# Experts of a fused attention and mixture kernel: side work, first weight fetches and last sums re-spaced

## The chip, the cores and the metric

The kernel runs on one core of one Trainium2 chip. The metric is device time in microseconds; the median of three runs of the kernel before is 872.75 us (871.38 to 873.23). Engines: PE (TensorE matmul), PEld (its weight loads), DVE (Vector), ACT (Scalar), POOL (GpSimd), SP (Sync, here the queue that issues DMAs).

## The reference

Three layers follow one another: gated linear attention over 4 x 8 heads of 768 steps, a mixture of 8 experts with equal capacity (3072 tokens, 384 each), and a dense layer with a cosine gate.

```python
def _moe_ref(x, w_gate, w1, w2):
    logits = x @ w_gate
    order = np.argsort(-logits.flatten())        # best (token, expert) pairs first
    # a pair is taken if the token is free and the expert has fewer than N // E tokens
    ...
    for e in range(E):
        mask = assigned == e
        h = np.maximum(x[mask] @ w1[e], 0.0)     # 384 -> 1024
        out[mask] = h @ w2[e]                    # 1024 -> 384

def _moe2_ref(x, w_in, w_out):
    h = x @ w_in                                 # 384 -> 2048
    g = h * np.cos(h)
    return (g @ w_out).astype(np.float32)        # 2048 -> 384
```

`w_in` and `w_out` are scaled with a numpy float64 and so reach the kernel as 64-bit floats; the kernel takes them as pairs of 32-bit words and makes float32 of them with integer operations.

## The kernel before

The kernel has three stages: attention (up to about 168 us in the profile), the search for the first full expert (up to about 180 us), and `experts`, which this change is about. The order in which experts fill up is found on the way: a search finds the next expert to be full and its threshold, and the tokens of that expert are then fixed. The kernel works through the experts in that order, 384 tokens at a time, and does the routing of the next expert beside the matmuls of the current one.

**Precision.** Every float32 product is three matmuls (`mm3`, lines 741 to 743, and lines 811 to 813): operands are split into a rounded high part (made on ACT, `..h`) and the rest (made on DVE or POOL, `..l`). A piece of work on PE in this text is nine matmuls of 128x384.

**One expert.** `prefetch` gathers the tokens with three indirect DMAs on POOL (line 706, one per 128 tokens), and fetches the first three of eight raw weight blocks on SP (line 716, three buffers). `convert` makes a block's high part on ACT (`wh`, line 723) and low part on POOL (`wl`, line 724; the first three of the first expert on DVE), and then fetches the block three further on. `xpose` transposes the tokens on PE (line 753). `up(f)` is the first product for block f of 1024/128 = 8 with its relu (`hh` on ACT, `hl` on DVE), `down(f)` the second, into `accB`. `up2(f)` is the third product for one of 16 blocks of 2048 with the cosine (ACT, DVE, ACT, DVE), then `gh` on ACT and `gl` on POOL (lines 800, 801), and `down2(f)` the last product into `accD`, which runs three blocks behind `up2`. The last `down2` of an expert copies `accD` out and scatters the rows with an indirect DMA on POOL (line 820).

**Side work.** The generator `beside` of expert n yields the routing of expert n + 1, its `prefetch` and its first five conversions, step by step. `tick` is called 42 times in an expert, after each piece of matmuls or so, and takes the next step on two calls of three. A search has six refinement steps k. In each, DVE compares all best logits with a list of thresholds (`C`, line 549, in two halves), PE counts (`cn`, line 545), DVE decides whether the capacity is reached (`less`, `sat`), PE adds up (`num`, line 572), and DVE makes the next thresholds (`thr`, lines 589 and 597). `C` and its count are one step of the generator, the decision and the new thresholds the next. Experts 0 to 5 have a search beside them (for experts 1 to 6); expert 6 has only the routing of the last expert, and expert 7 nothing. Behind the search come the ranks (`rk`, line 632), four comparisons `L` (line 661), their product `xi` (line 658) and the indices `idx` (line 675).

**Late weights.** Ten of the 16 blocks of `w_out` are converted during attention; the last six (`LATE`) beside the first expert by `convert_late`. Each has four steps: an absolute value on ACT (line 137), two operations on DVE (lines 139, 140), two more on DVE (142, 143), and the high part on ACT with the low part on POOL (146, 147). `next(late, None)` takes one step.

**What sets the order.** Program order is a priority. When the program is built, a planner simulates the engines with its own costs and gives every engine a fixed list: of the instructions that it takes to be ready, the earliest in program order. `in_order` pins an engine's list to program order: POOL and DVE in the lead-in of `experts`, ACT in the main loop. On the chip each engine works through its list and waits where an input is not there. The lead-in (from line 830) routes expert 0, calls `prefetch`, converts five blocks, keeps PE running with matmuls that nobody reads (`busy`, 22 in a row and two after each third of the transposes) and transposes.

Of the kernel before, what the change touches and what calls it, by code (L numbers as in the profile page):

```python
# [525 lines left out]
def search(nc, K, rp, ps, Z, n, em, found):  # L526
    V, PE = nc.vector, nc.tensor
    mx, oh = Z["mx"], Z["oh"]
    steps = FIRST if n == 0 else LATER
    thr, tau, old = K["t0"].bitcast(F32)[:, ::2 ** (steps[0] - 25)], None, None  # L530
    for k, st in enumerate(steps):
        T = 2 ** ((32 if k == 0 else steps[k - 1]) - st)
        g = P // T if n > 0 else 1
        if st:
            nx = steps[k + 1]
            wd = 2 ** (st - nx)
        if k == 0 and n == 0:
            cn = Z["cn"]
        else:
            C = rp.tile([P, NU, T], BF16, name="C", tag="C")  # L540
            cn = ps.tile([g * T, g * E], F32, name="cn", tag="rt")

            def count(a, z):
                for c in range(a, z, g):
                    PE.matmul(cn, C[:, c:c + g].rearrange("p c t -> p (c t)"), oh[:, c:c + g].rearrange("p c e -> p (c e)"), start=(c == 0), stop=(c == NU - g))  # L545

            cuts = (0, 15, NU) if n == 0 else tuple(range(0, NU + 1, HALF))
            for a, z in zip(cuts, cuts[1:]):
                V.tensor_tensor(C[:, a:z], mx[:, a:z, None].to_broadcast([P, z - a, T]), thr[:, None, :].to_broadcast([P, z - a, T]), op=ALU.is_ge)  # L549
                if n == 0:  # L550
                    count(a, z)
            if n > 0:
                count(0, NU)
            if st and k:
                base = rp.tile([P, wd], I32, name="base", tag="base")
                V.scalar_tensor_tensor(base, K["io"][:, :wd], nx, tau.to_broadcast([P, wd]), op0=ALU.logical_shift_left, op1=ALU.bitwise_xor)
            yield
        sat = rp.tile([T, E], BF16, name="sat", tag="sat")
        if g == 1:
            V.tensor_scalar(sat, cn, CAP - 0.5, None, op0=ALU.is_ge)  # L560
        else:
            less = None
            for j in range(1, g):
                part = cn[j * T:(j + 1) * T, j * E:(j + 1) * E]
                more, less = less, rp.tile([T, E], F32, name="less", tag="less", bufs=2)
                if j == 1:
                    V.tensor_scalar(less, part, -1.0, None, op0=ALU.mult)
                else:
                    V.scalar_tensor_tensor(less, part, -1.0, more, op0=ALU.mult, op1=ALU.add)
            V.scalar_tensor_tensor(sat, cn[:T, :E], 0.5 - CAP, less, op0=ALU.add, op1=ALU.is_ge)  # L570
        num = ps.tile([P, E], F32, name="num", tag="rt")
        PE.matmul(num, K["onesb" if st == 0 else "ones0"][:T], sat, start=True, stop=True)
        ix = rp.tile([P, 1], I32, name="ix", tag="ix")
        if st == 0:
            top = rp.tile([P, 1], F32, name="top", tag="top")
            V.tensor_reduce(top, num, axis=AX, op=ALU.max)
            sel = rp.tile([P, E], F32, name="sel", tag="sel")
            V.scalar_tensor_tensor(sel, num, top, K["eb"], op0=ALU.is_equal, op1=ALU.mult)
            V.tensor_reduce(em, sel, axis=AX, op=ALU.max)
            V.tensor_scalar(ix, top, -1.0, None, op0=ALU.add)  # L580
            V.tensor_tensor(found, ix, tau, op=ALU.bitwise_xor)
            yield
            break
        with nc.allow_low_precision(reason="small whole numbers"):
            V.tensor_reduce(ix, num, axis=AX, op=ALU.max)
        old, tau = tau, rp.tile([P, 1], I32, name="tau", tag="tau", bufs=2)
        if k:
            thr = rp.tile([P, wd], I32, name="thr", tag="thr", bufs=2)
            V.scalar_tensor_tensor(thr, ix.to_broadcast([P, wd]), st, base, op0=ALU.logical_shift_left, op1=ALU.bitwise_xor)
            V.scalar_tensor_tensor(tau, ix, st, old, op0=ALU.logical_shift_left, op1=ALU.bitwise_xor)  # L590
        else:
            t2 = rp.tile([P, 1], I32, name="t2", tag="t2i")
            V.tensor_scalar(tau, ix, st, -2**31, op0=ALU.logical_shift_left, op1=ALU.bitwise_xor)
            V.tensor_scalar(t2, tau, 31, 0x7FFFFFFF, op0=ALU.arith_shift_right, op1=ALU.bitwise_and)
            V.tensor_tensor(tau, tau, t2, op=ALU.bitwise_xor)
            thr = rp.tile([P, wd], I32, name="thr", tag="thr", bufs=2)
            V.scalar_tensor_tensor(thr, K["io"][:, :wd], nx, tau.to_broadcast([P, wd]), op0=ALU.logical_shift_left, op1=ALU.bitwise_xor)  # L597
        thr = thr.bitcast(F32)
        yield
    if n == 0:  # L600
        V.tensor_copy(Z["ems"], em)
    else:
        V.tensor_tensor(Z["ems"], Z["ems"], em, op=ALU.add)
# [84 lines left out]
def experts(tc, nc, ctx, K, R, Z, xs, wcat, wout, out):  # L688
# [13 lines left out]
    def prefetch(r):  # L702
        r["xg"] = []
        for j in range(3):
            t = mp.tile([P, HD], F32, name="xg", tag="xg", bufs=3)
            GP.indirect_dma_start(out=t, out_offset=None, in_=xs, in_offset=bass.IndirectOffsetOnAxis(ap=r["idx"][:, j:j + 1], axis=0))
            r["xg"].append(t)
        r["e"] = nc.sync.value_load(r["es"][0:1, 0:1], min_val=0, max_val=E - 1)
        r["raw"], r["w"] = {}, {}
        for f in range(3):  # L710
            fetch(r, f)

    def fetch(r, f):
        if f < NA:
            r["raw"][f] = mp.tile([P, 2 * HD], F32, name="raw", tag="raw", bufs=3)
            nc.sync.dma_start(r["raw"][f], wcat[bass.ds(r["e"], 1), :, f].rearrange("a p c -> p (a c)"))

    def convert(r, f, eng=None):
        if f < NA:
# [110 lines left out]
    late = convert_late(nc, mp, R, wout)  # L830
    next(late)
    cur = fresh()
    second = fresh()
    steps = route(nc, K, rp, rtp, Z, 1, second)
    with in_order(tc, nc, (mybir.EngineType.Pool, mybir.EngineType.DVE)):
        for _ in route(nc, K, rp, rtp, Z, 0, cur):
            pass
        prefetch(cur)
        for f in range(5):
            convert(cur, f, V if f < 3 else None)  # L840
        next(steps)
        cur["busy"] = mmp.tile([P, 512], F32, name="busy", tag="mm")
        busy(cur, 22)
        xpose(cur, 2)
        mark = {i.name for i in nc.cur_bb.bb.instructions}
    up(cur, 0)
    up(cur, 1)
    with in_order(tc, nc, (mybir.EngineType.Activation,)):
        for n in range(E):
# [3 lines left out]
            def beside():  # L853
                if nxt is not None:
                    if n == 0:
                        next(steps)
                        hold(tc, nc, mybir.EngineType.DVE, mark)
                        yield
                    yield from steps if n == 0 else route(nc, K, rp, rtp, Z, n + 1, nxt)
                    prefetch(nxt)  # L860
                    yield
                    for f in range(5):
                        convert(nxt, f)
                        yield
            side = beside()
            count = [0]

            def tick():
                count[0] += 1
                if count[0] % 3:  # L870
                    next(side, None)
            for f in range(2, NA):
                up(r, f)
                tick()
                down(r, f - 2)
                convert(r, f + 3)
                tick()
            for d in range(3):
                down(r, NA - 2, (d,))
# [6 lines left out]
            for f in range(LEAD, LAG):  # L886
                up2(r, f)
                next(late, None)
                tick()
                next(late, None)  # L890
            down2(r, (0,))
            tick()
            for f in range(LAG, NF):
                up2(r, f)
                next(late, None)
                tick()
                down2(r, (f - LAG + 1,))
                next(late, None)
                tick()
            for f in range(NF + 1 - LAG, NF - 2):  # L900
                down2(r, (f,))
                tick()
            for _ in side:
                pass
            if nxt is not None:
                xpose(nxt)
                down2(r, (NF - 2,))
                up(nxt, 0)
                up(nxt, 1)
                down2(r, (NF - 1,))  # L910
            else:
                down2(r, (NF - 2, NF - 1))
            cur = nxt


# [93 lines left out]
```

## Time and profile before

| | |
|---|---|
| median of 3 runs | 872.75 us |
| profiled execution | 871.95 us |
| its span | 870.2 us |
| PE busy | 810.0 us (93%) |
| DVE busy | 529.8 us (61%) |
| ACT busy | 423.8 us (49%) |
| POOL busy | 378.8 us (44%) |
| raw fetch, median from issue to landing | 3.4 us (64 of 384 KB) |

Busy time is the time in which the engine has an instruction running; matmuls overlap, so a busy PE is not yet PE at its peak. The granted clock of PE is full (2.4 GHz) or half of that (1.2 GHz); the views give it as a share. The times in the views count from the start of the span. In a row of a windows view the busy times stand in the order PE, PEld, DVE, ACT, POOL, each with its number of instructions.

### The profile page before, as it was taken

What the parts mean: (1) busy time and instruction counts of PE and PEld (TensorE: products, weight loads), DVE (VectorE), ACT (ScalarE), POOL (GpSimd) and SP (SyncE); (2) the same over time, 40 slices, a digit from 0 to 9 for tenths busy, and PEclk for the clock granted to TensorE, in tenths of its full rate; (3) what the DMA queues carried; (4) which work ended last, traced back from release to release, by engine and by line L of the source; (5) the groups of instructions that cost most, each with busy time, mean ns of one, the idle gap of its engine ahead of it and who ended that gap; (6) DMA issues with size and microseconds to landing.
All of it is one profiled execution on the core that took longest, in us unless ns stands there. A gap on an engine that the chain in (4) does not pass through costs nothing.

```text
span 870.2 us, 15619 instructions
## 1 busy us (share of the span) xinstructions
PE 810.0 (93%) x5886; PEld 760.0 (87%) x5886; DVE 529.8 (61%) x1365; ACT 423.8 (49%) x814; POOL 378.8 (44%) x329
## 2 busy tenths in 40 slices
PE   6989999648998899999999999999999999999996
PEld 4878889527988889999998999899989999999996
DVE  5888888565697368546844683567357645432332
ACT  4777776113355425632563356245624553753552
POOL 5545555013146513751384138314732563734233
PEclk9999999859999999999999999999999999999999
DMA  9988884142032201220131014002300133300000
GB/s 243 262 229 222 232 223 120 40 126 86 1 109 82 83 1 55 72 75 2 55 101 46 1 55 119 28 1 73 101 28 27 60 113 85 92 1 28 1 2 28
DMA packets 27348, 71.91 MB, mean 83 GB/s; under 512 B 4608, under 2 KB 7936, under 8 KB 27264
## 3 DMA queue, kind: packets, MB, share of 16 engines
q1 hardware_dynamic: 24192, 61.38, 24.7%
q0 software_dynamic: 3072, 9.44, 3.4%
q8 instruction: 49, 0.80, 0.4%
q14 instruction: 35, 0.29, 0.1%
HBM read 61.37 MB, written 9.44 MB: 81 GB/s over the span
## 4 chain that ended last, share of the span: by engine, by line
PE 47%; DVE 2%; ACT 1%; issue 0%; POOL 0%; POOLq 0%; ACTq 0%
PE accD L812 5%; PE accD L811 5%; PE accD L813 5%; PE pC L742 5%; PE pC L741 5%; PE pC L743 5%; PE accB L741 2%; PE pA L741 2%; PE accB L742 2%; PE accB L743 2%; PE pA L743 2%; PE pA L742 2%; DVE C L549 1%; DVE thr L597 1%; PE xtp L753 1%; PE cn L545 1%
## 5 line engine op out<-in xcount | busy, mean ns | idle before, releaser
L801 POOL TENSOR_TENSOR gl<-ki,gh 128x384 fp32r<-128x384 f32 x128 | 132.1, 1036 | 249.8 <-ACT gh L800 228.1
L813 PE MATMUL accD<-woh,gl 128*128 128x384 f32 x384 | 131.1, 341 | 5.6 <-POOL gl L801 5.6
L724 POOL TENSOR_TENSOR wl<-raw,wh 128x768 fp32r<-128x768 f32 x61 | 112.7, 1853 | 51.4 <-ACT wh L723 43.5
L811 PE MATMUL accD<-woh,gh 128*128 128x384 f32 x384 | 131.7, 343 | 0.5 <-ACT gh L800 0.5
L812 PE MATMUL accD<-wol,gh 128*128 128x384 f32 x384 | 130.9, 341 | 0.0
L743 PE MATMUL pC<-yTh,wil 128*128 128x384 f32 x384 | 130.3, 339 | 0.0
L741 PE MATMUL pC<-yTh,wih 128*128 128x384 f32 x384 | 130.0, 341 | 0.0
L742 PE MATMUL pC<-yTl,wih 128*128 128x384 f32 x384 | 129.9, 338 | 0.0
L787 DVE SCALAR_TENSOR_TENSOR ki<-pC,ki 128x384 f32<-128x384 f32 x128 | 71.0, 555 | 85.2 <-ACT ki L785 85.0
L785 ACT ACTIVATE ki<-pC,quarter 128x384 int32<-128x384 f32 x128 | 73.7, 576 | 92.2 <-PE pC L743 90.9
L792 DVE TENSOR_TENSOR ki<-pC,ki 128x384 f32<-128x384 f32 x128 | 71.0, 555 | 53.8 <-ACT ki L790 50.3
L790 ACT ACTIVATE ki<-ki,halfpi 128x384 f32<-128x384 f32 x128 | 79.0, 617 | 43.9 <-DVE ki L787 43.6
L732 ACT ACTIVATE hh<-pA 128x384 fp32r<-128x384 f32 x64 | 31.5, 492 | 114.9 <-PE pA L743 114.9
L723 ACT CAST wh<-raw 128x768 fp32r<-128x768 f32 x64 | 52.3, 828 | 61.6 <-PE accB L742 32.2
L813 PEld LDWEIGHTS accD<-woh,gl 128*128 128x128 f32 x384 | 72.7, 189 | 7.3 <-POOL gl L801 7.2
L733 DVE SCALAR_TENSOR_TENSOR hl<-pA,hh 128x384 fp32r<-128x384 f32 x64 | 35.5, 555 | 63.1 <-ACT hh L732 62.9
L811 PEld LDWEIGHTS accD<-woh,gh 128*128 128x128 f32 x384 | 72.8, 189 | 0.9 <-ACT gh L800 0.8
L742 PEld LDWEIGHTS pC<-yTl,wih 128*128 128x128 f32 x384 | 72.5, 189 | 0.6 <-DVE yTl L736 0.5
L800 ACT CAST gh<-ki 128x384 fp32r<-128x384 f32 x128 | 64.8, 506 | 16.8 <-DVE ki L792 16.6
L812 PEld LDWEIGHTS accD<-wol,gh 128*128 128x128 f32 x384 | 72.6, 189 | 0.0
L741 PEld LDWEIGHTS pC<-yTh,wih 128*128 128x128 f32 x384 | 72.5, 189 | 0.1
L743 PEld LDWEIGHTS pC<-yTh,wil 128*128 128x128 f32 x384 | 72.5, 189 | 0.0
(187 smaller groups left out, 1688.8 us busy)
## 6 DMA issues: line engine op xcount, KB each, us to landing
raw<-in_wcat_dram SPq DMA_DIRECT2D x64, 384.0 KB, 3.4
ring<-in_qk_dram SPq DMA_DIRECT2D x48, 192.0 KB, 5.0
vf<-in_qkvf_dram SPq DMA_DIRECT2D x23, 384.0 KB, 4.9
wr<-in_win_dram SPq DMA_DIRECT2D x12, 512.0 KB, 5.4
xs<-xx SPq DMA_DIRECT2D x24, 192.0 KB, 2.7
wr<-in_wout_dram SPq DMA_DIRECT2D x10, 384.0 KB, 4.8
lr<-in_wout_dram SPq DMA_DIRECT2D x6, 384.0 KB, 3.3
vf<-in_qkvf_dram SPq DMA_DIRECT2D x2, 192.0 KB, 3.2
```

The costliest lines, as they stand in the source:

```text
L724: (eng or GP).tensor_tensor(l, raw, h.bitcast(F32), op=ALU.subtract)
L741: PE.matmul(o, ah, bh, start=first, stop=False)
L742: PE.matmul(o, ah, bl, start=False, stop=False)
L743: PE.matmul(o, al, bh, start=False, stop=last)
L785: SC.activation(ki, p, AF.Identity, bias=quarter, scale=INV2PI)
L787: V.scalar_tensor_tensor(fr, p, INV2PI, ki, op0=ALU.mult, op1=ALU.subtract)
L790: SC.activation(fr, fr, AF.Sin, bias=halfpi, scale=TWO_PI)
L792: V.tensor_tensor(g, p, fr, op=ALU.mult)
L801: GP.tensor_tensor(gl, g, gh.bitcast(F32), op=ALU.subtract)
L811: PE.matmul(r["accD"][t], gh[:, s], R["oh"][:, f], start=(f == 0), stop=False)
L812: PE.matmul(r["accD"][t], gh[:, s], R["ol"][:, f], start=False, stop=False)
L813: PE.matmul(r["accD"][t], gl[:, s], R["oh"][:, f], start=False, stop=(f == NF - 1))
```

## The change

- In `search`, a step with n > 0 yields once more, between `C` and its count.
- `tick` takes a side step on every call. A conversion in `beside` yields twice.
- In the first expert, fetches of raw blocks 3 and later (`fetch`, f >= 3) wait for the third gather. SP issues them.
- Two of the steps of `convert_late` now come with each block of the up and down loop, and one, not two, with each block of up2. The number of calls up to block 12 of up2 is 24 in both versions.
- 18 instead of 22 `busy` matmuls stand ahead of the transposes.
- In the last expert, `down2` of block 13 is no longer a call by itself: blocks 13, 14 and 15 are summed in one call, all three for the first 128 tokens, then for the second, then for the third.

```diff
@@ search
                 if n == 0:
                     count(a, z)
             if n > 0:
+                yield
                 count(0, NU)
             if st and k:
                 base = rp.tile([P, wd], I32, name="base", tag="base")
@@ prefetch, fetch
         for j in range(3):
             t = mp.tile([P, HD], F32, name="xg", tag="xg", bufs=3)
-            GP.indirect_dma_start(out=t, out_offset=None, in_=xs, ...)
+            got = GP.indirect_dma_start(out=t, out_offset=None, in_=xs, ...)
             r["xg"].append(t)
         r["e"] = nc.sync.value_load(r["es"][0:1, 0:1], min_val=0, max_val=E - 1)
         r["raw"], r["w"] = {}, {}
         for f in range(3):
             fetch(r, f)
+        if r.get("wait"):
+            r["wait"] = got.ins
 
     def fetch(r, f):
         if f < NA:
             r["raw"][f] = mp.tile([P, 2 * HD], F32, name="raw", tag="raw", bufs=3)
-            nc.sync.dma_start(r["raw"][f], wcat[...])
+            d = nc.sync.dma_start(r["raw"][f], wcat[...])
+            if f >= 3 and r.get("wait"):
+                info = mybir.DependencyInfo(mybir.DependencyClass.Sync, mybir.DependencyReason.DATA)
+                tc.add_manual_dep(d.ins, r["wait"].name, info, reason="gathers first")
@@ lead-in
     cur = fresh()
+    cur["wait"] = True
...
-        busy(cur, 22)
+        busy(cur, 18)
@@ main loop
                     for f in range(5):
                         convert(nxt, f)
                         yield
+                        yield
             side = beside()
-            count = [0]
 
             def tick():
-                count[0] += 1
-                if count[0] % 3:
-                    next(side, None)
+                next(side, None)
             for f in range(2, NA):
                 up(r, f)
+                next(late, None)
                 tick()
                 down(r, f - 2)
                 convert(r, f + 3)
+                next(late, None)
                 tick()
...
                 up2(r, f)
                 next(late, None)
                 tick()
-                next(late, None)
             down2(r, (0,))
             tick()
             for f in range(LAG, NF):
                 up2(r, f)
                 next(late, None)
                 tick()
                 down2(r, (f - LAG + 1,))
-                next(late, None)
                 tick()
-            for f in range(NF + 1 - LAG, NF - 2):
+            for f in range(NF + 1 - LAG, NF - 2 if nxt is not None else NF - 3):
                 down2(r, (f,))
                 tick()
...
             else:
-                down2(r, (NF - 2, NF - 1))
+                down2(r, (NF - 3, NF - 2, NF - 1))
```

## Rows read from the trace of the kernel before

**Rows 1.** Windows by expert (first, third): stretch, length, busy us (instructions), clock, DMA share, GB/s.
```profile
200.77:293.41 92.64, 84.67 (x501) 79.10 (x501) 67.20 (x167) 44.99 (x85) 41.12 (x34) 0.96 0.22 66
376.36:459.62 83.26, 81.53 (x510) 77.60 (x510) 50.34 (x141) 38.70 (x71) 36.73 (x30) 1.00 0.18 53
```

**Rows 2.** Windows: late stretch of the first and third expert, then the first's up stretch.
```profile
263.39:290.84 27.45, 21.64 (x101) 20.01 (x100) 17.76 (x24) 16.05 (x30) 20.88 (x17) 0.88 0.35 100
439.76:457.05 17.29, 17.29 (x100) 17.26 (x100) 6.14 (x11) 12.44 (x22) 16.50 (x14) 1.00 0.46 127
...
200.50:228.00 27.50, 26.50 (x174) 24.26 (x174) 17.99 (x51) 7.19 (x13) 6.41 (x4) 1.00 0.10 29
```

**Rows 3.** Waits of PE from 200 us on: us in total, times, longest.
```profile
PE cn L545 <- DVE C L549: 7.4, 7, 1.3
PE accD L813 <- POOL gl L801: 5.6, 4, 2.8
PE rk L632 <- DVE R L630: 0.6, 1, 0.6
```

**Rows 4.** Timeline, third expert: start, us, engine, line, operation, [idle before, releaser].
```profile
388.68 1.84 POOL L724 TENSOR_TENSOR wl<-raw,wh 128x768 fp32r<-128x768 f32 x1 [1.70 <-ACT wh L723]
...
388.83 1.77 DVE L597 SCALAR_TENSOR_TENSOR thr<-io,tau 128x64 int32<-128x64 int32 x1
...
389.64 0.33 PE L741 MATMUL accB<-hh,wh 128*128 128x384 f32 x1
...
390.63 1.83 DVE L549 TENSOR_TENSOR C<-mx,thr 128x768 bf16<-128x768 f32 x2
391.64 0.31 PE L545 MATMUL cn<-oh,C 128*128 128x16 bf16 x6 [1.32 <-DVE C L549]
...
393.20 0.35 PE L741 MATMUL pA<-xTh,wh 128*128 128x384 f32 x1
```

**Rows 5.** Timeline of PE, third expert, around two later counts.
```profile
397.21 0.34 PE L743 MATMUL pA<-xTh,wl 128*128 128x384 f32 x1
397.60 0.24 PE L545 MATMUL cn<-oh,C 128*128 128x32 bf16 x3
...
415.79 0.34 PE L813 MATMUL accD<-woh,gl 128*128 128x384 f32 x1
416.23 0.24 PE L545 MATMUL cn<-oh,C 128*128 128x32 bf16 x3
```

**Rows 6.** Line 597, the thresholds: count, ns min/median/max, first and last start, forms.
```profile
L597 DVE SCALAR_TENSOR_TENSOR thr<-io,tau x7: 193/1769/1775, 168.1 to 638.1; 128x64 int32<-128x64 int32 x6, 128x32 int32<-128x32 int32 x1
```

**Rows 7.** Tile `lv`, the late blocks' DVE steps: count, ns min/median/max.
```profile
L139 DVE TENSOR_SCALAR lv<-lv x6: 342/350/1090, 237.8 to 274.6; 128x384 f32<-128x384 f32 x6
L140 DVE TENSOR_SCALAR lv<-lv x6: 339/346/1867, 238.3 to 275.7; 128x384 int32<-128x384 int32 x6
L142 DVE SCALAR_TENSOR_TENSOR lv<-lr,lv x6: 543/932/1261, 239.1 to 277.6; 128x384 int32<-128x384 int32 x6
L143 DVE SCALAR_TENSOR_TENSOR lv<-lr,lv x6: 536/543/545, 240.1 to 279.3; 128x384 int32<-128x384 int32 x6
```

**Rows 8.** Timeline of the lead-in; a later gather; the window after that.
```profile
192.33 9.23 SPq L716 DMA_DIRECT2D raw<-in_wcat_dram  x5
...
194.30 1.08 POOL L706 DMA_INDIRECT xg<-xs,idx  x1 [0.30 <-issue]
...
199.65 0.55 PE L753 MATMUL xtp<-ident,xg 128*128 128x128 f32 x3 [0.22 <-DMA xg<-xs,idx]
...
689.05 0.95 POOL L706 DMA_INDIRECT xg<-xs,idx  x1 [0.30 <-ACT ki L790]
...
692.00:693.00 1.00, 1.00 (x8) 1.00 (x7) 0.56 (x1) 0.82 (x2) 0.51 (x2) 1.00 0.00 0
```

**Rows 9.** Timeline of the end.
```profile
859.49 1.01 POOL L801 TENSOR_TENSOR gl<-ki,gh 128x384 fp32r<-128x384 f32 x1 [1.02 <-ACT gh L800]
...
860.55 0.44 PE L813 MATMUL accD<-woh,gl 128*128 128x384 f32 x1 [0.26 <-POOL gl L801]
```

More of the change, by code (lines that the diff above doesn't have):

```diff
@@ L705, in prefetch @@
             t = mp.tile([P, HD], F32, name="xg", tag="xg", bufs=3)
-            GP.indirect_dma_start(out=t, out_offset=None, in_=xs, in_offset=bass.IndirectOffsetOnAxis(ap=r["idx"][:, j:j + 1], axis=0))
+            got = GP.indirect_dma_start(out=t, out_offset=None, in_=xs, in_offset=bass.IndirectOffsetOnAxis(ap=r["idx"][:, j:j + 1], axis=0))
             r["xg"].append(t)
@@ L715, in fetch @@
             r["raw"][f] = mp.tile([P, 2 * HD], F32, name="raw", tag="raw", bufs=3)
-            nc.sync.dma_start(r["raw"][f], wcat[bass.ds(r["e"], 1), :, f].rearrange("a p c -> p (a c)"))
+            d = nc.sync.dma_start(r["raw"][f], wcat[bass.ds(r["e"], 1), :, f].rearrange("a p c -> p (a c)"))
+            if f >= 3 and r.get("wait"):
+                info = mybir.DependencyInfo(mybir.DependencyClass.Sync, mybir.DependencyReason.DATA)
+                tc.add_manual_dep(d.ins, r["wait"].name, info, reason="gathers first")
     def convert(r, f, eng=None):
```

## The prediction

> **What bounds the kernel now.** The chain of waits and the windows by expert come first. From 200 us on the time is TensorE's: in the expert stretches PE is busy almost throughout, so only its idle time and its clock can be won. An expert with a search beside it takes 83.26 us, the first one 92.64 us [rows 1], although the first has nine closing matmuls fewer. The second view cuts that excess down to its place: the last eleven pieces of the first expert take 27.45 us where the same eleven take 17.29 us in the third, at a mean clock of 0.88 against 1.00 [rows 2]: 10.2 us. There POOL is busy 20.88 us and DVE 17.76 us, against 16.50 and 6.14. The third view, PE's waits after 200 us, names what ends the idle time: counts waiting for C (7.4 us, seven times) and closing matmuls waiting for POOL's `gl` (5.6 us, four times, all in the first expert) [rows 3]. The timeline of the third expert then shows why a count waits [rows 4, 5], and that of the lead-in why expert 0 starts at 200.77 us [rows 8].
>
> **The timetable.** An expert calls `tick` 42 times: 12 in the up and down loop, one after it, 3 before `down2(0)`, one after, 24 in the main up2 loop, one at the end. Before, two ticks of three advance the side work (28 steps, 26 needed with a search). After, all 42 do and 37 steps are needed: 26, six for the new yield, five for the second yield per conversion. For experts 1 to 5 a search step took C and count on one tick, then an empty tick or the decision; now it takes C, count, decision on three. So each C and each decision stays on its old tick, the count alone goes one tick (nine matmuls) later. Behind the search the four L pieces stand on ticks 21 to 24 instead of 22 to 26, the gathers on 27 instead of 31, the five conversions on 28, 30, 32, 34, 36 instead of 32, 34, 35, 37, 38.
>
> **Counts, experts 1 to 5.** In step 1 the thresholds (`thr`) take 1.77 us, since POOL's `wl` began 0.15 us earlier; the first search, with POOL silent, has the same line at 0.19 us (half as wide) [rows 4, 6]. C is complete 1.83 us after 390.63, at 392.46. PE came to the first half of the count after three matmuls of `down(2)` and stood from about 390.16 to 391.64: 1.48 us. Both halves now stand behind all nine: PE arrives at 389.64 + 9 x 0.174 = 391.21, waits for the first half until 391.64 and for the second until about 392.54, and `up(5)` begins near 392.70 instead of 393.20. Gain 0.50; about 1.1 us of idle stays, because neither `thr` nor `wl` moves. The two smaller waits (397.21 + 0.17 to 397.60, 0.21 us; 415.79 + 0.17 to 416.23, 0.27 us) end before a count that is nine matmuls later, and go [rows 5]. That is 0.98 an expert, five experts: **-4.9 us**. Bounds: 0 (the planner keeps the places) to 1.96 x 5 = 9.8 (all idle gone). A decision now follows its count by one tick instead of two; expert 0 had that spacing all along, and its decisions appear in no wait of 0.5 us among those of rows 3. The denser L pieces cost nothing while `gl` keeps its slack: it is used three up2/down2 pairs later.
>
> **The first expert's late stretch.** Six blocks of w_out need four steps each, 24 calls. Before, they came two per up2 from block 1, all beside the sine chain. Now twelve calls lie in the up loop (three blocks done there), three in up2 blocks 1 to 3 and nine in blocks 4 to 12; the last call stays where it was, but only one falls on each block. The stretch loses one of its three POOL subtractions and half of its Vector steps, and the five `wl` (1.84 us each [rows 4]) stand one per up2/down2 pair instead of bunched. POOL then holds 1.84 + 1.01 for `gl` [rows 4, 9] in a pair of 18 x 0.174 = 3.1 us. The third expert does the same bunched, at 16.50 of 17.29 us of POOL, and stalls nowhere in it [rows 2]. With no idle there the clock stayed at 1.00 throughout. Of 10.2 us I take **-8.5**, leaving 1.7 for the gathers and two remaining subtractions meeting the first `wl`. Bounds: -10.2 and 0. Earlier in up2, PE's wait for R at `rk` (0.6 us [rows 3]) comes from the same crowding: **-0.6**, bounds 0 and -0.6.
>
> **The first expert's up stretch** pays. In 27.5 us DVE is busy 17.99 and POOL 6.41 [rows 2]. Three blocks bring 0.34 + 0.34 + 0.54 + 0.54 = 1.76 us of Vector each at the shortest, 5.3 us in all, 23.3 of 27.5; at the longest seen (1.09, 1.87, 1.26, 0.55) 4.77 each, 14.3 us, 32.3 of 27.5 [rows 7]. POOL gets three subtractions of `gl`'s shape, 1.0 each, and the `wl` of raw 3 and 4, which now come after the gathers. Two ACT instructions per block stand in ACT's pinned order between the relu copies; a copy that waits for a slow Vector step holds back the next `hh`, which has two pieces of slack. The planner knows the work but, judging by where it put the counts, not the collisions. Low end -0.4, high end 32.3 - 27.5 = +4.8; I take **+1.4**, nearer the undisturbed durations, since the medians of three of the four lines lie within 0.01 us of the shortest.
>
> **The lead-in.** The third gather is issued at 194.30 and its transposes run at 199.65, 5.35 us later, while raw fetches start from 192.33 on [rows 8]. An undisturbed third gather, issued at 689.05, has all traffic over by 692, 2.95 us later [rows 8]. Allowing 0.4 us from the last traffic to the transposes, that is 3.35 instead of 5.35: **-2.0**, bounds -2.4 and +3.5 (a rival). The wait sits on SP: raw 3, 4, 5 queue behind it, then 6 and 7, whose slots need `wl` 3 and 4. Fetches land in 3.4 us by the page's part 6; raw 3 at about 201, its conversion by 203.8, before `up(3)` at about 206, so that delay is hidden; if not, each us late costs one. The four `busy` matmuls removed stood before the first gather landed: nothing, but if the clock fell to half there, the 27 matmuls of `up` 0 to 2 would take 27 x 0.174 = 4.7 us more. Expert 0's first count moves with the rest.
>
> **The end.** `down2` of blocks 13, 14, 15 by token group leaves 27 matmuls and the same last operand, `gl` of block 15, ready at 860.50, for which PE stood until 860.55 [rows 9]. If the planner fills from other groups, nothing changes; if not, 18 matmuls instead of 12 follow that wait, 1.04 us, of which the three scatters' own spacing hides over half. Between 0 and +1.0: **+0.2**.
>
> **Sum.** -4.9 - 8.5 - 0.6 + 1.4 - 2.0 + 0.2 = -14.4. The profiled execution took 871.95 us (span 870.2), 0.80 below the median 872.75; so 857.55 there, **858.4** as a median. The measurement tells about 0.2%, 1.75 us, from no change.
>
> **Rivals.** (1) POOL stays the bound of the late stretch: gathers, `gl`, `wl` and two subtractions leave it no gap, and 3 us instead of 8.5 come back: 863.9. For it: 16.50 of 17.29 us without any late work. Against it: that stretch never stalled.
> (2) All idle goes, the threshold collision included: -9.8 - 9.7 - 0.6 - 0.4 - 2.4 = -22.9, 849.9. Against it: nothing moves `wl` or `thr` in experts 1 to 5.
> (3) The planner leaves ACT's conversions of raw 3 and 4 ahead of the copies of the transposes: `up(0)` waits for raw 4 (about 202.5), two casts and the copy, to about 204.3, +3.5 instead of -2.0: 863.9.
> (4) The yield doesn't do what it says, the planner issues counts where it did: 863.3.
> (5) Slower: Vector is kept out by POOL in the first expert's up stretch. `thr` shows the mechanism: one operation beside `wl` cost 1.58 us more, the median of seven [rows 6]. Twelve moved Vector operations, eight C halves and four thresholds, 24, now stand beside eight POOL operations there, and each count and decision of the search, and each `hl`, queues behind them on DVE. The other terms give -15.8 in all, so it decides from 15.8 / 24 = 0.66 us a piece; at 0.9 it costs 21.6 and the kernel takes 878.6. Against it: the same operations beside `gl` and `wl` had medians of 0.35, 0.35, 0.93 and 0.54 [rows 7], a mean excess near 0.1.
> The Trainium skill's page SBUF — State Buffer, section "SBUF: two separate sides", says of this that Vector operations with two SBUF inputs or in a two-port mode and GpSimd share a port pair as an exclusive lock, held for a whole instruction, whoever starts first. Taken at its worst, every one of the 24 could by that rule wait for a whole POOL operation, and rival 5 would be the forecast; the medians in this trace agree with the rule only for those that meet one.
>
> **Chances.** Forecast 0.54, rivals 1 to 5: 0.14, 0.10, 0.07, 0.07, 0.08. Mixtures of gains given back, within 0.2%, have 0.06 of the forecast's and the rivals' weight left, so that slower is 0.08, same 0.06, faster 0.86. The range 851 to 866 holds the forecast (its own range 854 to 862) and rivals 1, 3 and 4; left out are rival 5, the mixtures and about half of rival 2, 0.19.
>
> **What will show it.** The first expert's window should fall from 92.6 to about 85, its late stretch to 19 us with clock 1.00; if POOL is still at 20 us there, rival 1. In experts 1 to 5 the second count should stand behind nine `accB` matmuls, one piece of twelve, still waiting about 1.1 us with `thr` at 1.77; two pieces would be rival 4, no wait rival 2. The Vector lines of the late blocks (`lv`) with means over 1 us and PE idle in 200 to 228 would be rival 5. `up(0)` should start at 198.8, ACT's copies of the transposes ahead of its fourth cast. The prediction is wrong if the first expert's window does not fall by 5 us, or if up(0) is later than now.

## The result and the profile after

The changed kernel takes 859.75 us (median of 4 runs, 858.61 to 860.28), the kernel before 872.34 us beside it (4 runs): a ratio of 0.9852, 95% interval 0.9822 to 0.9882. 858.4 was predicted, range 851 to 866. The profiled execution took 859.24 us, its span 856.7. The total came out well; its largest term did not, nor did the test that I had set for it.

Windows by expert (first, third), then the late stretch (last eleven pieces) and the up stretch of the first expert, all after the change. Columns as in [rows 1]: stretch, length, busy us of PE, PEld, DVE, ACT, POOL, clock, DMA share, GB/s.

```profile
196.37:285.46 89.09, 82.37 (x500) 75.86 (x501) 72.11 (x167) 46.40 (x87) 45.60 (x35) 1.00 0.28 82
367.31:449.18 81.87, 81.02 (x510) 77.87 (x510) 49.55 (x141) 39.03 (x71) 36.86 (x30) 1.00 0.18 54
...
261.63:282.92 21.29, 18.32 (x101) 17.01 (x101) 14.12 (x22) 13.93 (x26) 15.79 (x13) 1.00 0.34 94
196.37:223.90 27.53, 24.79 (x162) 22.38 (x163) 23.56 (x54) 10.94 (x21) 12.34 (x7) 1.00 0.33 100
```

The first expert fell from 92.64 to 89.09 us, the third from 83.26 to 81.87 [rows 1]; the late stretch fell from 27.45 to 21.29 and kept full clock [rows 2]. In it POOL is busy 15.79 of 21.29 us: it has gaps now, and PE still stands 3 us. In the up stretch PE stands 2.7 us, and Vector is busy 23.56 of 27.53 us.

The first expert's gain is less waiting only in part. PE's idle time there (length less busy time) only fell from 7.97 to 6.72 us; its busy time fell from 84.67 to 82.37 us, as the clock rose from 0.96 to 1.00. In the late stretch alone idle fell by 2.8 and busy time by 3.3 us, at 0.88 and then 1.00.

The two spans differ by 13.6 us (870.24 and 856.68). Put together from the starts of the experts in the two traces:

| Where | predicted | measured |
|---|---|---|
| ahead of the gathers, code unchanged | 0 | -2.1 |
| lead-in, third gather's issue to `up(0)` | -2.0 | -2.3 |
| first expert, late stretch | -8.5 | -6.2 |
| first expert, the rest (up stretch +1.4, `rk` -0.6) | +0.8 | +2.6 |
| experts 1 to 5 | -4.9 | -5.6 |
| end | +0.2 | 0.0 |
| sum | -14.4 | -13.6 |

The -2.1 us belong to no edit. The profiled execution of before has a stretch at half clock from 16.71 to 20.12 us in the attention stage, the one after has none, and other executions of changed and unchanged kernels fall on either side: the third gather is issued at 194.30 in before and 194.95 in e3, at 192.19 in after and 192.22 in e2. Without it the profiles differ by 11.5 us, the medians by 12.6.

PE's waits from the first expert on, after the change (us in total, times, longest), against [rows 3]:

```profile
PE cn L545 <- DVE C L549: 5.2, 12, 0.7
PE accD L819 <- POOL gl L807: 2.5, 3, 1.7
PE num L573 <- DVE sat L571: 2.0, 2, 1.6
PE accD L817 <- ACT gh L806: 0.8, 1, 0.8
```

Counts wait less in all, `gl` less than half as long, and a wait that was 0.5 us in all before stands third: the decision's `num` waits for `sat`, both times in the first expert.

**The count.** Timeline of the third expert's step 1, against [rows 4]:

```profile
379.63 1.84 POOL L730 TENSOR_TENSOR wl<-raw,wh 128x768 fp32r<-128x768 f32 x1 [1.71 <-ACT wh L729]
379.78 1.78 DVE L598 SCALAR_TENSOR_TENSOR thr<-io,tau 128x64 int32<-128x64 int32 x1
380.60 0.33 PE L747 MATMUL accB<-hh,wh 128*128 128x384 f32 x1
...
381.60 1.83 DVE L549 TENSOR_TENSOR C<-mx,thr 128x768 bf16<-128x768 f32 x2
382.61 0.31 PE L545 MATMUL cn<-oh,C 128*128 128x16 bf16 x6 [0.29 <-DVE C L549]
383.48 0.31 PE L545 MATMUL cn<-oh,C 128*128 128x16 bf16 x6 [0.56 <-DVE C L549]
383.64 0.43 PE L747 MATMUL pA<-xTh,wh 128*128 128x384 f32 x1
```

As predicted: `wl` and `thr` collide as before, `thr` takes 1.78 us, the count stands behind nine `accB` matmuls and still waits, 0.29 + 0.56 = 0.85 us instead of 1.32 and more.

**The lead-in.** Timeline after the change, against [rows 8]:

```profile
192.19 0.95 POOL L707 DMA_INDIRECT xg<-xs,idx  x1 [0.30 <-issue]
195.25 0.55 PE L759 MATMUL xtp<-ident,xg 128*128 128x128 f32 x3 [0.28 <-DMA xg<-xs,idx]
195.61 1.24 ACT L741 CAST xTh<-xtp 128x384 fp32r<-128x384 f32 x3 [4.94 <-PE xtp L759]
199.10 1.79 ACT L729 CAST wh<-raw 128x768 fp32r<-128x768 f32 x2 [2.24 <-DMA raw<-in_wcat_dram]
```

From the third issue to its transposes it is 3.06 us (5.35 before, 3.35 forecast), and ACT copies the transposes ahead of the casts of raw 3 and 4.

**The first expert's up stretch.** Timeline of DVE, POOL and PE around the new wait:

```profile
204.38 2.17 POOL L730 TENSOR_TENSOR wl<-raw,wh 128x768 fp32r<-128x768 f32 x1 [0.71 <-ACT wh L729]
205.00 1.97 DVE L143 SCALAR_TENSOR_TENSOR lv<-lr,lv 128x384 int32<-128x384 int32 x1
...
207.00 0.16 DVE L571 SCALAR_TENSOR_TENSOR sat<-cn,less 64x8 bf16<-64x8 f32 x1
207.21 0.18 PE L573 MATMUL num<-sat,ones 64*128 64x8 bf16 x1 [1.61 <-DVE sat L571]
```

The late step L143 starts beside `wl` and takes 1.97 us (0.55 at the shortest). `sat` is behind it on Vector and PE stands 1.61 us for `num`. A second piece, L142 at 213.68 with 2.14 us, delays a count by 0.7.

**Its late stretch.** Timeline ahead of and in it:

```profile
257.67 1.50 POOL L707 DMA_INDIRECT xg<-xs,idx  x1 [0.16 <-issue]
258.72 4.48 DVE L226 TENSOR_TENSOR w<-w,eb 128x192 f32<-128x192 f32 x1
259.19 1.03 POOL L147 TENSOR_TENSOR wol<-lv,woh 128x384 fp32r<-128x384 f32 x1
260.17 1.84 POOL L730 TENSOR_TENSOR wl<-raw,wh 128x768 fp32r<-128x768 f32 x1
261.98 1.01 POOL L807 TENSOR_TENSOR gl<-ki,gh 128x384 fp32r<-128x384 f32 x1
264.00 0.54 DVE L793 SCALAR_TENSOR_TENSOR ki<-pC,ki 128x384 f32<-128x384 f32 x1
264.57 0.62 ACT L796 ACTIVATE ki<-ki,halfpi 128x384 f32<-128x384 f32 x1 [5.23 <-DVE ki L793]
...
266.44 1.81 POOL L730 TENSOR_TENSOR wl<-raw,wh 128x768 fp32r<-128x768 f32 x1 [3.45 <-ACT wh L729]
266.48 2.19 DVE L142 SCALAR_TENSOR_TENSOR lv<-lr,lv 128x384 int32<-128x384 int32 x1
...
268.22 1.31 POOL L807 TENSOR_TENSOR gl<-ki,gh 128x384 fp32r<-128x384 f32 x1
...
269.58 0.44 PE L819 MATMUL accD<-woh,gl 128*128 128x384 f32 x1 [1.66 <-POOL gl L807]
```

`w` is the next search's, hoisted into this stretch by the planner; elsewhere it takes 0.36 us. Here it starts beside POOL's third gather and ends 0.2 us after the last of four POOL operations on end (261.98 + 1.01 = 262.99; 258.72 + 4.48 = 263.20). Behind it the sine chain's `ki` is late, ACT stands 5.23 us, and PE stands three times, 2.96 us in all, for `gh` and `gl` between 266.5 and 273.46. The late step L142 at 266.48 adds to it with 2.19 us, but is held in another way: it ends 0.42 us after the one POOL operation that it met (266.44 + 1.81 = 268.25; 266.48 + 2.19 = 268.67), while POOL goes on with `gl` until 269.53.

**The end.** Timeline, against [rows 9]:

```profile
847.00 0.44 PE L819 MATMUL accD<-woh,gl 128*128 128x384 f32 x1 [0.35 <-POOL gl L807]
```

The same operand, `gl` of block 15, ends it, with nearly the same wait (0.35 us, 0.26 before); expert 7 to the end takes 84.84 us (84.86 before).

### The profile page after: what moved, and what is told of

Same layout as the page of the kernel before. It is cut to its first block, busy times and chain, and to the rows that moved or that the text cites. A ratio compares the mean times of both kernels' runs of the same rounds, so it can differ in the third digit from the quotient of the medians.

```text
span 856.7 us, 15606 instructions
## 1 busy us (share of the span) xinstructions
PE 801.8 (94%) x5880; PEld 756.1 (88%) x5882; DVE 530.2 (62%) x1365; ACT 425.2 (50%) x814; POOL 380.8 (44%) x329
## 4 chain that ended last, share of the span: by engine, by line
PE 66%; DVE 8%; DMA 1%; issue 1%; ACT 1%; POOL 1%; SPq 0%; POOLq 0%; DVEq 0%; ACTq 0%
PE pC L747 7%; PE pC L749 7%; PE accD L817 7%; PE accD L819 7%; PE pC L748 7%; PE accD L818 7%; PE accB L747 4%; PE pA L747 3%; PE accB L749 3%; PE accB L748 3%; PE pA L749 3%; PE pA L748 3%; DVE C L549 2%; DVE thr L598 1%; DMA raw<-in_wcat_dram 1%
## 5 line engine op out<-in xcount | busy, mean ns | idle before, releaser
L793 DVE SCALAR_TENSOR_TENSOR ki<-pC,ki 128x384 f32<-128x384 f32 x128 | 70.9, 554 | 85.6 <-ACT ki L791 85.0
```

The costliest lines, as they stand in the source:

```text
L793: V.scalar_tensor_tensor(fr, p, INV2PI, ki, op0=ALU.mult, op1=ALU.subtract)
```

## The experiments

Three questions: which part brought what (e1 to e3), what holds the first expert back (e4 to e6), and whether that can be had (e7 to e12). "First expert" is the window from its `up(0)` to the next expert's.

**e1, e2: the parts alone.** e1 is the kernel before with the side work's edits of `search` and `tick` and the second yield; e2 is the kernel before with the calls of `late` moved and nothing else.

```
e1   +                yield                      (ahead of count(0, NU))
     -                if count[0] % 3:           (every tick advances)
     +                        yield              (second one per conversion)
e2   +                next(late, None)           (twice in the up loop)
     -                next(late, None)           (one of two in each up2 loop)
```

> The kernel before with the re-spaced side work alone (the yield ahead of the counts, tick on every call, two yields per conversion); late blocks, lead-in and end as before. Theory (the parts add up, each in its own place): experts 1 to 5 fall from 83.0 to 81.9 us each, 5.6 in all, and the first expert keeps 91.5 to 93, because its late blocks still stand two calls to a pair: ratio about 0.993, some 866 us. Rival (the first expert's gain came from the conversions standing one to a pair, not from the late blocks): its window is near 89 and the time near 863.

> The kernel before with the late blocks of w_out re-spaced alone (twelve calls in the up loop, one per up2 after it). Theory (each part in its own place): first expert 89 us, its last eleven pieces 21 us, experts 1 to 5 still 83 each: ratio 0.996, some 869 us. Rival (re-spaced late blocks only move the trouble into the up stretch unless the conversions are spread too): first expert 91 or more, ratio 0.999 or above.

e1: 865.57 us, ratio 0.9922 (0.9899 to 0.9945). e2: 866.14, 0.9937 (0.9915 to 0.9960). Windows of the first and the third expert, e1 and then e2:

```profile
204.94:296.06 91.12, 83.19 (x501) 77.31 (x502) 69.76 (x166) 44.45 (x83) 43.33 (x34) 0.98 0.21 63
377.92:459.85 81.93, 81.08 (x511) 77.87 (x510) 49.53 (x141) 38.93 (x71) 36.88 (x30) 1.00 0.18 54
```
```profile
199.38:287.38 88.00, 83.31 (x500) 78.65 (x501) 64.91 (x167) 45.29 (x85) 42.44 (x34) 0.96 0.22 66
370.34:453.31 82.97, 81.49 (x511) 77.59 (x510) 50.35 (x141) 38.73 (x71) 36.74 (x30) 1.00 0.18 53
```

The parts stand in their own places: the side work alone brings experts 1 to 5 all of their 5.5 us (409.4 against 414.9; e2 leaves 414.8), the late blocks alone bring the first expert 4.6 and the side work 1.5. Together they bring 3.6 in after and 4.4 in e3: here they do not add. In the rows PE's idle time in the first expert is 7.93 us in e1 and 4.69 in e2, against 7.97 before and 6.72 after: the late blocks alone take 3.3 us of idle away, and with the side work beside them 2 us of it come back.

**e3: the old lead-in in the changed kernel.**

```
-    cur["wait"] = True
...
-        busy(cur, 18)
+        busy(cur, 22)
```

> The changed kernel without the wait of the raw fetches on the gathers and with busy at 22. Theory (the wait is worth 2.2 us, the other 2.2 us of the profiled difference of 4.4 at up(0) arose in the attention stage, whose code is the same): up(0) 2 to 2.5 us later after the gathers' issue, time 862.0, ratio to before 0.988. Rival (the gathers' traffic isn't slowed by the raw fetches, the whole 4.4 us is between executions): time 859.8, ratio 0.9855, third gather to transposes near 3 us without the wait too.

861.46 us, 0.9883 (0.9858 to 0.9907); the interval overlaps that of after, so the time alone does not tell. The timeline does:

```profile
194.95 0.95 POOL L707 DMA_INDIRECT xg<-xs,idx  x1 [0.30 <-issue]
200.38 0.83 ACT L729 CAST wh<-raw 128x768 fp32r<-128x768 f32 x1 [2.80 <-DMA raw<-in_wcat_dram]
201.53 0.55 PE L759 MATMUL xtp<-ident,xg 128*128 128x128 f32 x3 [1.31 <-DMA xg<-xs,idx]
201.90 1.24 ACT L741 CAST xTh<-xtp 128x384 fp32r<-128x384 f32 x3 [0.68 <-PE xtp L759]
```

6.58 us from the third issue to the transposes. Over four executions of the old lead-in, issue to `up(0)` took 6.47 (before), 8.55 (e1), 7.16 (e2) and 7.71 (e3); over ten with the wait, 4.16 to 4.62. The wait is worth 2.3 us or more. The figure of e1 holds some half clock as well (0.57 from 201 to 203 us; PE stood 3.00 us for a gather until 201.55). e3 puts back the four `busy` matmuls too, but its third transposes wait 1.31 us for the gather, and not for PE.

**e4, e5, e6: what in the late blocks costs.** Vector's four steps and POOL's subtraction of the six late blocks, left out together (e4) and one at a time (e5 the steps, e6 the subtraction). e4 has both edits:

```
-            V.tensor_scalar(...)          (and the three steps after it)
-        GP.tensor_tensor(R["ol"][:, f], r, R["oh"][:, f].bitcast(F32), op=ALU.subtract)
+        nc.scalar.copy(R["ol"][:, f], r)
```

> The changed kernel with the late blocks' four Vector steps left out and POOL's subtraction replaced by a copy on ScalarE; blocks 10 to 15 of w_out are then only the absolute value of the half word, in both parts. It asks how much of the first expert's 89.1 us is due to the late blocks at all. Theory (late blocks put Vector operations with two operands in SBUF and POOL subtractions beside each other, and each waits for the other): first expert near 82, time 852.5, ratio 0.977. Rival (the rest is the next search hoisted beside the gathers, and would be there without late blocks): first expert 87 or more, time 857 or more.

> The changed kernel whose late blocks keep ScalarE's two copies and POOL's subtraction but skip the four Vector steps (blocks 10 to 15 of w_out are then the absolute value of the half word). With e4 (neither; first expert 80.22 us against 89.09) it makes a square: Vector steps or not, POOL's subtraction or not. Theory (each stands in the other's way: Vector steps behind POOL): most of the 8.9 us goes with either of the two, first expert 81 to 84, and no Vector line takes over 2.5 us in its late stretch except the hoisted w and C. Rival POOL-bound (POOL has too much to do, rival 1 of the prediction): first expert stays at 86 or more, since POOL keeps all its work. Rival Vector-full: 80 to 81.

> The changed kernel whose late blocks keep all Vector steps, while POOL's six subtractions are replaced by a copy on ScalarE (the low parts of blocks 10 to 15 then hold a copy of the value instead). Theory (Vector steps behind POOL): first expert 82 to 85; the steps still meet wl and gl. Rival POOL-bound: 80 to 81, everything goes with POOL's six subtractions. Rival Vector-full: 87 or more, since Vector keeps all its work.

850.77 us (0.9762, 0.9738 to 0.9787), 852.91 (0.9789, 0.9766 to 0.9812) and 858.64 (0.9870, 0.9841 to 0.9899). Windows of the first expert, e4, e5, e6:

```profile
196.48:276.69 80.21, 79.94 (x500) 76.33 (x501) 53.36 (x143) 48.70 (x93) 38.39 (x29) 1.00 0.30 92
```
```profile
198.28:280.16 81.88, 80.55 (x501) 76.30 (x501) 57.62 (x143) 46.32 (x87) 44.56 (x35) 1.00 0.30 90
```
```profile
196.71:283.69 86.98, 82.07 (x501) 75.95 (x502) 70.02 (x167) 48.86 (x93) 39.49 (x29) 1.00 0.28 84
```

With neither, the first expert is clean: 80.21 us, near the third's 81.87 less nine matmuls of 0.174. All three rows are at full clock, as is after's. So all of the 8.9 us left in after are the late blocks'. Vector's steps cost 7.2 with POOL's subtractions there (89.09 - 81.88) and 6.8 without (86.98 - 80.21); the subtractions 2.1 and 1.7. The costs nearly add. My theory, that either edit takes most away, holds for e5 and fails in e6, which stands at the edge of its Vector-full rival; Vector's side carries about four fifths. POOL as a bound is refuted: e5 keeps all its work, 44.56 us, and takes 81.88. e5 also has one Vector operation (`oh`, L228) kept for 4.60 us behind POOL, and PE shows no wait for it: without the late steps Vector, it seems, has the slack.

**e7: the late subtraction on Vector.**

```
-        GP.tensor_tensor(R["ol"][:, f], r, R["oh"][:, f].bitcast(F32), op=ALU.subtract)
+        V.tensor_tensor(R["ol"][:, f], r, R["oh"][:, f].bitcast(F32), op=ALU.subtract)
```

> The changed kernel with the late blocks' low part (the subtraction for wol) on Vector instead of POOL: the whole computation, six operations of 128x384 moved, 0.35 to 0.55 us each on Vector in place of 1.0 on POOL. Theory (Vector behind POOL): first expert 84 to 87, time 855 to 858, faster than the changed kernel. Rival Vector-full: first expert 90 or more, time 861 or more. Rival POOL-bound: as good as e6.

858.97 us, 0.9857 (0.9838 to 0.9876); first expert 87.81. No Vector-full result, but hardly the theory's either: level with after. In time it is as good as e6, which was the POOL-bound rival's sign; but the first expert is 0.8 us longer than e6's, and e5 speaks against POOL as a bound.

**e8: one more yield ahead of the count of step 1.**

```
-                yield
+                yield from range(1 + (k == 1))
```

> The changed kernel with a second yield ahead of the count of step 1 of a later search, so that this count alone goes one more tick back. In experts 2 to 5 PE still waits for C 3.4 us in eight waits, two an expert, all in that step, beside POOL's wl. Theory (the wait is only a matter of place): the waits go, experts 1 to 5 take 81.0 us each instead of 81.87, time 855.5 to 857. Rival (the decision that follows comes a tick later too, and the next count waits in its place, or the conversions, now at the end of the 42 ticks, are late): 81.8 or more an expert, time 859 to 862.

863.07 us, 0.9908 (0.9892 to 0.9924). The rival is right: that wait goes, a later count waits 0.6 an expert in its place, and an expert takes 81.95. The first expert grows to 91.90, with a decision that waits 2.4 us and a clock of 0.98, so the time lies above the rival's too.

**e9, e10, e11: moving the victims.** e9 holds the next search's first Vector operations behind the first expert's last one; e10 starts the late blocks three calls later; e11 has both.

```
e9   +                    if n == 1:
     +                        next(it)
     +                        hold(tc, nc, mybir.EngineType.DVE, over)
     ...
e10  -                next(late, None)
     +                next(late, None) if f > 3 else None
     ...
```

> The changed kernel in which the Vector operations that open the third expert's search (best expert and the first C, hoisted into the last stretch of the first expert, among them w at 258.72 with 4.48 us in place of 0.36) are held behind the last Vector operation of that stretch. Theory (delays of Vector beside POOL reach TensorE only where Vector has no slack; there w and C took it): TensorE's stalls at 267.29, 269.58 and 273.46 go, 3.45 us: first expert 85.6, time 856.3. Rival (the late steps beside wl would stall there anyway, or the second expert's count pays for the late start): first expert 88 or more, or second expert 83 or more, time 859 or more.

> The changed kernel with the late blocks starting three calls later (no call in the pair of f = 2 and one in that of f = 3, three more in up2 13 to 15). Theory (the first expert pays in its first pairs, where a late Vector step met wl of raw 3 and 4): the stalls at 201.92, 207.21 and 216.98 go, 3.0 us, and up to 1 us comes back later: first expert 86 to 87, time 857 to 858. Rival (it is Vector's total load: the same loss shows up in other places): first expert 88.5 to 90, time 859.5 to 861.

> Both edits of e9 and e10. If their places are independent the gains add: first expert 82.5 to 84, time 853.5 to 855, the lower end being what e5 reached without any late Vector step (81.88). Rival (they fight over the same slack of Vector): no better than the better of the two.

e9: 857.34 us, 0.9834 (0.9811 to 0.9857): first expert 86.76, 2.3 less than after and between the theory's 85.6 and the rival's 88, second 82.70, 0.8 more. e10: 859.64 (0.9860, 0.9836 to 0.9883), first expert 90.23. e11: 861.75 (0.9877, 0.9853 to 0.9902), 89.42 and 82.80. e9 is the best whole version, by 1.5 us in the traces; its interval overlaps that of after. The hold moved `w` away, and another operation took its place, in the timeline of e9:

```profile
259.43 5.95 DVE L139 TENSOR_SCALAR lv<-lv 128x384 f32<-128x384 f32 x1
259.57 1.84 POOL L730 TENSOR_TENSOR wl<-raw,wh 128x768 fp32r<-128x768 f32 x1
...
264.16 1.00 POOL L807 TENSOR_TENSOR gl<-ki,gh 128x384 fp32r<-128x384 f32 x1
```

POOL runs without a gap until 265.16, L139 until 265.38. In e10 and e11 the rivals hold by the time: the stall at 207.21 goes, and PE stands 2.50 us at a decision some seven us later. I had taken these for separate stalls to be removed one by one; in these runs another Vector operation is caught each time. But e10's loss is not idle time. Window of its first expert:

```profile
196.51:286.74 90.23, 84.60 (x501) 78.58 (x501) 70.87 (x167) 46.17 (x87) 45.59 (x35) 0.96 0.28 81
```

PE's idle time is 5.63 us in e10, 1.1 less than in after, the way that the theory went; its busy time is 2.2 us longer, at a clock of 0.96 and not 1.00. The clock is 0.71 from 213 to 215 us and 0.50 from 215 to 217, and the 2.50 us in which PE stood end at 214.33; it is low again from 281 to 287.

**e12: the late steps with a PSUM operand.** e7 with `lv` in PSUM, beside the search's small tiles in their bank.

```
-            v = stg.tile([P, HD], I32, name="lv", tag="lv", bufs=2)
+            v = ps.tile([P, HD], I32, name="lv", tag="lv")
...
```

> e7 (low part of the late blocks on Vector) with the late blocks' values (lv) held in PSUM, in the bank of the search's small tiles, instead of SBUF: the same computation and the same Vector operations, but each now has a PSUM operand, like the sine chain's ki<-pC,ki, which took 0.55 to 0.56 us beside POOL all through e5, e6 and e9. The planner puts some counts of the first expert elsewhere. Theory (a Vector operation whose operands all lie in SBUF waits for POOL's whole burst, and that is what the late steps cost): no line of the late steps takes over 0.9 us, first expert 82.5 to 85.5 against 87.80 in e7, time 854 to 856.5. What is left is the hoisted w. Rival (Vector has simply too much to do in the first expert; where its operands lie doesn't matter): first expert 87 or more, time 858 or more. Rival from the shared bank: the steps wait for the counts' readers, stalls at lv in new places, first expert over 88.

861.57 us, 0.9887 (0.9864 to 0.9909); first expert 90.29. Lines of the late steps, 190 to 296 us (busy us, mean ns), e7 and then e12:

```profile
L147 DVE TENSOR_TENSOR wol<-lv,woh 128x384 fp32r<-128x384 f32 x6 | 8.4, 1399 | 0.0
L143 DVE SCALAR_TENSOR_TENSOR lv<-lr,lv 128x384 int32<-128x384 int32 x6 | 5.4, 892 | 0.0
```
```profile
L139 DVE TENSOR_SCALAR bank<-bank 128x384 f32<-128x384 f32 x6 | 3.4, 559 | 1.3 <-PE bank L545 1.1 <-ACT wh L729 0.3
L143 DVE SCALAR_TENSOR_TENSOR bank<-lr,bank 128x384 int32<-128x384 int32 x6 | 3.3, 558 | 0.0
L147 DVE TENSOR_TENSOR wol<-bank,woh 128x384 fp32r<-128x384 f32 x6 | 3.3, 552 | 1.4 <-ACT woh L146 1.4
```

That the operand's place decides is shown: with a PSUM operand all five lines take 552 to 559 ns in the mean, where the same lines in SBUF took up to 1399. Of the 30 operations 12 began while POOL ran, and none took over 0.57 us; of the 24 in after, in SBUF, seven took over 0.6 us, and all seven began while POOL ran. The time went the other way, as both rivals have it. Windows of the first expert, e7 and then e12:

```profile
198.29:286.10 87.81, 81.72 (x501) 75.85 (x501) 73.76 (x173) 46.37 (x87) 41.81 (x29) 1.00 0.29 84
```
```profile
197.51:287.80 90.29, 83.72 (x500) 77.14 (x501) 69.75 (x173) 45.89 (x87) 37.47 (x29) 0.98 0.28 81
```

Of the 2.5 us between them 2.0 are busy time, at the lower clock, and 0.5 idle. The hoisted C stands in POOL's burst instead, timeline of e12:

```profile
264.94 5.64 DVE L549 TENSOR_TENSOR C<-mx,t 128x768 bf16<-128x768 f32 x1
...
268.02 0.66 PE L819 MATMUL accD<-woh,gl 128*128 128x384 f32 x1 [2.96 <-POOL gl L807]
```

and the shared bank adds waits of its own (L139 1.1 us for the counts). PE's 2.96 us ahead of 268.02 fall together with the clock (0.77 from 267 to 269 us, 0.50 from 269 to 271). So e12 settles which operations are stretched, and leaves open what the first expert would take if none were stretched.

## Why the prediction was right, and where it failed

**Counts, -4.9: right**, -5.6, by the predicted mechanism, and by that part alone (e1). One reason that the sum was low: the wait left is 0.85 us and not 1.1. Rival 4 is refuted, rival 2 too: the collision of `thr` and `wl` is still there.

**Lead-in, -2.0: right**, -2.3 in the profiled pair, and the runs say that the old one was often worse. Rival 3 had it backwards: it is the old order in which ACT casts raw 4 ahead of the copies (e3, 200.38 ahead of 201.90), and even there ACT still waits 0.68 us for the transposes, so it costs nothing.

**End, +0.2:** 0.0. Three matmuls more than before follow the last wait (16 against 13); the first scatter starts 1.32 us after it in both, and the scatters' own spacing of 1.3 us hides the rest.

**The first expert is where it failed.** I forecast 85 us and wrote that less than 5 us of fall would make the prediction wrong; it fell by 3.6. The step that failed is "Of 10.2 us I take -8.5, leaving 1.7 for the gathers and two remaining subtractions meeting the first `wl`", and with it the up stretch's +1.4. I priced POOL's crowding as POOL's work, by the third expert, which "stalls nowhere in it". But the third expert has no late Vector steps: 6.14 us of DVE in that stretch [rows 2] against 14.12 in the first after the change. e5 with POOL's full work and no late steps has no wait for `gl` left; the steps themselves are the cost, 7 us. The clock came back as forecast, though 3 us of idle stayed; the prediction had tied the one to the other ("With no idle there the clock stayed at 1.00 throughout.").

**Rival 5 had the mechanism and not the price.** I gave it 24 operations at 0.66 us each and took comfort in medians near the shortest. My sign for it came true: L142 has a mean of 1.09 us and PE stands in the up stretch. The medians of three of the four lines are still near the shortest (L139 352 ns, L140 360, L142 558; L143 718 against 546); it is the few that count: L143 1.97, L142 2.14 and 2.19, `w` 4.48. A price per piece is the wrong form. A late step in SBUF that began beside `wl`, `wol` or `gl` in after waited until the POOL operation that it met had ended, as L142 at 266.48 did; the one exception began within 0.03 us of it (L140 at 236.31, 0.34 us). The few operations that took 3.7 us and more (one each in after, e3, e5 to e9, e11 and e12) paid for a whole run of POOL operations; in after, e5 and e9 they ended 0.2 us past its last. Each of these runs had begun with a gather. What decides between the two is not shown: in e1 `oh` at 267.80 started in such a run as well, and ended 0.2 us after the first operation that it met. The second yield per conversion did not shorten that burst; three gathers, `wol`, `wl` and `gl` still follow each other.
The Trainium skill, SBUF — State Buffer, section "SBUF: two separate sides", has the rule behind rival 5: the port pair shared by GpSimd and Vector operations with two SBUF inputs or in a two-port mode is locked for a whole instruction by whoever starts first. These runs agree on who is caught: `ki<-pC,ki` kept 0.55 us beside POOL, the late steps did too once in PSUM. On how long they agree for L142 at 266.48, and not for `w`: read one instruction at a time, `w` would have waited for the gather that ran, 0.45 us (257.67 + 1.50 - 258.72), and it waited until the fourth operation had ended.

**Why the total held:** the shortfall in the first expert, 4.2 us, was met up to 0.9 us by the counts (0.7), the lead-in (0.3), the end (0.2) and 2.1 us in the attention stage, which no edit touches. That is luck, and none of it was forecast. By the medians, which are freer of that, the miss is 1.35 us.

**Left open:** how much of the 7 us is Vector kept out and how much plain load on a Vector that is busy 23.56 of 27.53 us. e12 was to tell and brought new waits with it. The stalls shown, 1.61 us at 207.21, 0.73 and 0.23 behind L142 at 213.68, and 2.96 in the late stretch, make 5.5 of PE's 6.72 us of idle in the first expert, and each stands behind an operation that was held; that speaks for the first, and no run has the load without the holding at an equal clock.

## What to carry to other kernels

Before moving work onto a second engine's free time, ask which operations on the first cannot run beside it, and read the longest of each line and not the median: four held operations stand ahead of 5.5 of PE's 6.72 us of idle here. Ask too where the operand lies; a PSUM operand kept Vector at its own pace here. Look at the clock before calling a longer time a wait: in e10's first expert PE stood less than in after's, and it took longer. And check the sum term by term against the profile: a total within 0.2% hid a first expert that brought less than half of what I had forecast for it.

## What the runs showed of the hardware

A Vector operation of 0.35 us took 4.48 us (`w`, after), 4.60 (`oh`, e5), 4.95 (`oh`, e6) and 5.95 (L139, e9), each time beside three or more POOL operations on end. L142 (after, 266.48), beside `wl` with `gl` behind it, took 2.19 us and ended 0.42 after `wl`, with `gl` still running. L139 has a single SBUF input, so it isn't only operations with two. With raw weight fetches from SP's queue beside the three gathers, the third gather's transposes ran 5.35 (before), 6.03 (e2) and 6.58 us (e3) after its issue; with the fetches held back, 3.06 us (after): 2.3 to 3.5 us less.
